# Two fused layers on one core: casts and copies of the first two units go to ScalarE, weight slabs move forward in the GpSimd queue, and the order table is replaced

## The chip, the cores and the metric

The kernel runs on one core of a Trainium2 chip. The metric is the device time of one execution in microseconds; lower is better. Besides plain timed runs there is one execution under the hardware profiler, from which all views of the trace come.

## The reference

The program computes a retention layer for 8 batches and 8 heads (576 positions, head dimension 64) and, on its output, a feed-forward layer with the gate h·cos(h).

```python
scores = scale * np.matmul(q, k.transpose(0, 1, 3, 2))
gamma = 1.0 - 2.0 ** (-5.0 - np.arange(H, dtype=np.float32))
Dmat = np.where(rel >= 0, gamma[:, None, None] ** rel[None, :, :], 0.0)
ret = scores * Dmat[None, :, :, :]
attn_out = np.matmul(ret, v)            # [8, 8, 576, 64]
x = attn_out.transpose(0, 2, 1, 3).reshape(4608, 512)
h = x @ w_in                            # [4608, 2048]
out = (h * np.cos(h)) @ w_out           # [4608, 512], float32
```

## The kernel before

**Tiles.** A unit (b, g) is batch b with positions 256·g to 256·g+255 (g = 0, 1); the last 64 positions of four batches together form a unit (x, 2). The units are worked in pairs: (0,0), (1,0), then (0,1), (1,1), then (2,0), (3,0) and so on. Each pair gives one block of 512 tokens for the feed-forward layer; there are nine blocks, j = 0 to 8.

**Attention of a unit.** SyncE loads q, k and v as float32 into `stgq`, `stgk`, `stgv` (L585, 512 KB each for the units spoken of here). Then k is cast to bf16 (`natk`, L574 on ScalarE, L575 on VectorE or GpSimd), and q and v are multiplied by decay factors while they are cast (`qnat`, `natv`, L624). Each of the three comes as two halves, y = 0 and y = 1, of 128x512 elements. For the first two pairs of units TensorE transposes `natk` and `qnat` in four-matmul groups against the identity (L648), and ScalarE or VectorE copies the result out of PSUM into `kt` and `qt`. Later units are transposed by DMA (L663). TensorE makes the scores (`bk<-qt,kt`, L694), VectorE masks them (`pt`, L743), TensorE multiplies them with `natv` (`bk<-pt,natv`), adds the product of the queries with a running 64x64 state (`bk<-qt,sba`), and updates the state (`bk<-natv,natk`). The output is copied to `xt`.

**Feed-forward.** The first product of block 0 is a sequence of four-matmul groups (L908) over the four column slabs of `w_in`, taken in the order 0, 2, 1, 3; slabs 0 and 2 are done for each half of the block apart (256 columns), slabs 1 and 3 for both halves at once (512 columns). ScalarE makes the cosine (`cb`), VectorE the product (`gt`). The second product (L1177), and the first one of blocks 3 to 8 (L1037), use a scheme with seven products of sub-blocks instead of eight.

**Weight slabs.** GpSimd requests the slabs with DMAs that convert to bf16 (`win`, L888; `wout`, L892). Each has a gate: slab 0 of `w_in` waits until q of (0,0) has landed, slab 2 until q of (1,0) has, slabs 1 and 3 until k of (1,0) has. The loads of unit (0,1) wait until slab 2 has landed. The four slabs of `w_out` wait for k of unit (1,1), and the loads of (2,0) wait for one of them.

**What sets the order.** Every step is a task on one engine. A string, `ORDER`, gives each task a rank; on each engine the tasks run in the order of rank. A planner (`Graph.run`) walks through the tasks with assumed durations. [...] `SHARES` and `FETCH` are such assumptions: shares of the DMA engines when both kinds of queue are active, and the delay with which a block of TensorE instructions becomes usable.

**The first units.** In `unit`, a unit with `fast` set, which holds for (0,0) and (1,0), casts half 0 of k on ScalarE and half 1 on GpSimd. In the loop over `tpe`, the transposed tiles of half 0 are copied by ScalarE and those of half 1 by VectorE, if the unit is fast or stands in `BOTH`; otherwise ScalarE copies all.

## Time and profile before

| | us |
|---|---|
| median of 3 runs | 283.97 |
| lowest, highest | 283.41, 285.73 |
| profiled execution | 284.13 |
| its span, first to last instruction | 282.4 |
| TensorE busy | 270.7 (96%) |
| VectorE, ScalarE, GpSimd busy | 227.3, 177.5, 161.2 |

A row of a timeline gives the start, the duration, the engine, the line, the operation with its output and inputs, the count of merged instructions, and in brackets the idle time of the engine before it with what ended that idle time. PE is TensorE's matmul, PEld its weight load, DVE is VectorE, ACT ScalarE, POOL GpSimd, SP SyncE; a q behind the name marks the engine's sequencer, which waits and issues DMAs. "issue" means that the engine waited for nothing that the profile shows. In a table of windows each row is a stretch of time with each engine's busy time and instruction count, the granted TensorE clock, the busy share of the DMA engines (it can exceed 1, since packets overlap) and what they moved in GB/s.

### The profile page before, as it was taken

What the parts mean: (1) busy time and instruction counts of PE and PEld (TensorE: products, weight loads), DVE (VectorE), ACT (ScalarE), POOL (GpSimd) and SP (SyncE); (2) the same over time, 40 slices, a digit from 0 to 9 for tenths busy, and PEclk for the clock granted to TensorE, in tenths of its full rate; (3) what the DMA queues carried; (4) which work ended last, traced back from release to release, by engine and by line L of the source; (5) the groups of instructions that cost most, each with busy time, mean ns of one, the idle gap of its engine ahead of it and who ended that gap; (6) DMA issues with size and microseconds to landing.
All of it is one profiled execution on the core that took longest, in us unless ns stands there. A gap on an engine that the chain in (4) does not pass through costs nothing.

```text
span 282.4 us, 9745 instructions
## 1 busy us (share of the span) xinstructions
PE 270.7 (96%) x4136; PEld 219.9 (78%) x4136; DVE 227.3 (80%) x394; ACT 177.5 (63%) x367; POOL 161.2 (57%) x180
## 2 busy tenths in 40 slices
PE   6779989999999999979999999999999999999995
PEld 2457568888885468868888888888888888888884
DVE  3666889988974998868997996688759899997764
ACT  4346767255247765669469875885778865778530
POOL 4640872167377683897568757981375667216330
DMA  7999999999999999999999997979816090410016
GB/s 199 249 192 262 273 171 163 300 243 263 179 187 245 204 264 206 181 221 176 251 192 208 279 238 134 168 194 175 194 32 123 6 163 2 159 69 0 2 74 224
DMA packets 122731, 49.91 MB, mean 177 GB/s; under 512 B 84800, under 2 KB 118592, under 8 KB 122688
## 3 DMA queue, kind: packets, MB, share of 16 engines
q1 hardware_dynamic: 118176, 44.84, 74.8%
q0 software_dynamic: 4224, 4.19, 9.6%
q8 instruction: 32, 0.52, 0.8%
q10 hardware_dynamic: 288, 0.26, 0.3%
q14 instruction: 11, 0.09, 0.1%
HBM read 36.70 MB, written 9.44 MB: 163 GB/s over the span
## 4 chain that ended last, share of the span: by engine, by line
PE 84%; DMA 8%; POOL 3%; issue 2%; SPq 1%; DVE 1%; ACT 1%; DVEq 0%; ACTq 0%
PE bk L1177 38%; PE bk L1037 26%; PE bk L908 11%; PE bk L694 8%; DMA stgq<-in_q_dram 3%; DMA win<-in_moe_w_in_dram 3%; DMA stgk<-in_k_dram 3%; POOL natv L624 1%; SPq L585 1%; POOL qnat L624 1%; POOL gt L1026 1%; POOL win L888 0%; ACT xt L574 0%; DVE sq L1020 0%; PE bk L648 0%
## 5 line engine op out<-in xcount | busy, mean ns | idle before, releaser
L1026 POOL TENSOR_TENSOR gt<-sq,cb 128x512 bf16<-128x512 f32 x48 | 55.8, 1172 | 49.1 <-ACT cb L1022 27.0
L908 PE MATMUL bk<-xt,win 128*128 128x256 bf16 (+1 forms) x288 | 46.3, 308 | 1.8 <-DMA win<-in_moe_w_in_dram 0.9
L624 POOL TENSOR_TENSOR natv<-stgv,wv 128x512 bf16<-128x512 f32 x36 | 37.5, 1046 | 12.5 <-DVE s L1108 4.8
L920 DVE TENSOR_TENSOR gt<-bk,cb 128x256 bf16<-128x256 f32 (+1 forms) x72 | 34.5, 507 | 12.0 <-ACT cb L917 9.3
L917 ACT ACTIVATE cb<-bk 128x256 bf16<-128x256 f32 (+1 forms) x72 | 31.2, 455 | 19.6 <-PE bk L908 16.5
L624 POOL TENSOR_TENSOR qnat<-stgq,wq 128x512 bf16<-128x512 f32 x32 | 33.5, 1052 | 16.7 <-DVE s L1114 5.6
L1037 PE MATMUL bk<-xt,win 128*128 128x256 bf16 x288 | 41.0, 273 | 0.0
L1020 DVE TENSOR_TENSOR sq<-bk,sq 128x512 f32<-128x512 f32 x48 | 32.5, 684 | 8.9 <-PE bk L1037 5.0
L908 PEld LDWEIGHTS bk<-xt,win 128*128 128x128 bf16 x288 | 26.8, 98 | 15.3 <-DVE pt L743 1.2
L743 DVE TENSOR_TENSOR pt<-bk,tr 128x512 bf16<-128x512 f32 x48 | 31.1, 682 | 8.4 <-PE bk L694 8.1
L575 POOL CAST natk<-stgk 128x512 bf16<-128x512 f32 x34 | 20.7, 614 | 28.2 <-DMA stgk<-in_k_dram 15.7
L1177 PE MATMUL bk<-wout,gt 128*128 128x256 bf16 x288 | 36.7, 273 | 0.0
L1026 DVE TENSOR_TENSOR gt<-bk,cb 128x512 bf16<-128x512 f32 x48 | 32.3, 682 | 4.0 <-ACT cb L1022 3.8
L1177 PE MATMUL bk<-wout,s 128*128 128x256 bf16 x288 | 35.6, 273 | 0.0
L1177 PE MATMUL bk<-tw,s 128*128 128x256 bf16 x288 | 35.4, 273 | 0.0
L574 ACT ACTIVATE sq<-bk 128x512 f32<-128x512 f32 x48 | 27.7, 595 | 10.0 <-PE bk L1037 8.8
L1022 ACT ACTIVATE cb<-sq 128x512 bf16<-128x512 f32 x48 | 30.0, 632 | 5.4 <-DVE sq L1020 2.9
L1022 ACT ACTIVATE cb<-bk 128x512 bf16<-128x512 f32 x48 | 28.4, 598 | 6.7 <-PE bk L1037 3.7
L1177 PEld LDWEIGHTS bk<-tw,s 128*128 128x128 bf16 x288 | 28.0, 98 | 3.6 <-DVE pt L743 0.3
L1037 PEld LDWEIGHTS bk<-xt,win 128*128 128x128 bf16 x288 | 27.9, 98 | 3.6
L1177 PEld LDWEIGHTS bk<-wout,gt 128*128 128x128 bf16 x288 | 27.6, 98 | 3.7 <-issue 0.2
L1177 PEld LDWEIGHTS bk<-wout,s 128*128 128x128 bf16 x288 | 27.7, 98 | 3.5
(80 smaller groups left out, 436.5 us busy)
## 6 DMA issues: line engine op xcount, KB each, us to landing
stgq<-in_q_dram SPq DMA_DIRECT2D x16, 512.0 KB, 6.1
out_dram<-os SPq DMA_DIRECT2D x16, 512.0 KB, 4.4
stgk<-in_k_dram SPq DMA_DIRECT2D x20, 256.0 KB, 5.6
stgv<-in_v_dram SPq DMA_DIRECT2D x20, 256.0 KB, 5.4
stgk<-in_k_dram SPq DMA_DIRECT2D x6, 512.0 KB, 6.9
stgv<-in_v_dram SPq DMA_DIRECT2D x6, 512.0 KB, 7.4
win<-in_moe_w_in_dram POOLq DMA_DIRECT2D x4, 512.0 KB, 8.0
wout<-in_moe_w_out_dram POOLq DMA_DIRECT2D x4, 512.0 KB, 7.5
```

What stands on the lines that cost most here:

```text
L574: return self.one(eng, dur, lambda e: e.activation(dst(), src(), AF.Copy), r=r, w=w, **kw)
L624: self.one(eng, 610 if eng == "dve" else 1030, lambda e, out=out, inp=inp, tab=tab, col=col, hs=hs: e.tensor_tensor(out(), inp(), ap(tab, ...
L694: return lambda e: e.matmul(out(), lhs(), rhs(), start=start, stop=True, skip_group_check=True)
L743: self.one("dve", 610, lambda e, r=r, b=b, pt=pt: e.tensor_tensor(ap(self.at(pt), 1024, 0, 128, 512 * r, [64 * ny * ny, 8 // ny // ny], [1 ...
L908: inst = e.matmul(ap(self.at(bk), 512, 0, 128, 0, [1, n]), ap(self.WIN, 4 * DFF, 0, 128, c * DFF + 128 * f, [1, 128]), ap(self.at(xt), 204 ...
L917: self.one("act", n - 15, lambda e: e.activation(ap(self.at(cb), TB, 0, 128, 0, [1, n]), ap(self.at(bk), 512, 0, 128, 0, [1, n]), AF.Sin, ...
L920: self.one("dve", 75 + n / 0.96, lambda e: e.tensor_tensor(ap(self.at(gt), NF * TB, 0, 128, f * TB + 256 * h0, [1, n]), ap(self.at(bk), 51 ...
L1020: self.one("dve", 610, lambda e: e.tensor_tensor(half(src), self.at(bank).ap(), half(src), ALU.add), r=[(bank,)], w=four(src))
L1022: self.one("act", 530 if name else 490, lambda e: e.activation(self.at(cb).ap(), ap(self.at(src), size, 0, 128, 0, [1, 512]), AF.Sin, bias ...
L1026: self.one(eng, 1120 if name else 610, lambda e: e.tensor_tensor(ap(self.at(gt), NF * TB, 0, 128, (8 * n + 2 * g) * TB + 256 * h, [TB, 2], ...
L1037: inst = e.matmul(ap(self.at(bank), 512, 0, 128, 256 * f, [1, 256]), l(c, f), rr(c), stop=True, skip_group_check=True, start=(first and f ...
L1177: inst = e.matmul(place(bank, tt), l(f, tt), rr(f), stop=True, skip_group_check=True, start=(first and f == 0 and tt < len(bank)))
```

## The change

Half 1 of k of the two fast units is cast on ScalarE instead of GpSimd. `BOTH` now lists (0,0) and (0,1), and being fast no longer counts: so the four transposed tiles of (1,0) are all copied by ScalarE, while those of (0,0) and (0,1) remain shared between ScalarE and VectorE as before. The planner's assumptions on DMA shares, slab durations and instruction fetches are changed, and the whole order table is replaced.

```diff
-    BACKLOG, FIRST = 4000, 6000
-    SHARES = (0.65, 0.30)
-    FETCH = (3200, 1500, 2550, 2000)
+    BACKLOG = 4000
+    SHARES = (0.80, 0.42)
+    FETCH = ((8000, 3200, 0, 3550), (45000, 3200, 1500, 5050), (1e9, 3200, 1500, 3250))
...
-                    usable[k] = max(a + self.FETCH[0], dma_free + self.FETCH[1]) + self.FETCH[2] + self.FETCH[3] * (a < 45000)
+                    x, y, z = next(w for end, *w in self.FETCH if a < end)
+                    usable[k] = max(a + x, dma_free + y) + z
...
     ORDER = (
-        "#####$#$#$#%#%#$#######%#&#&#%#$#&#'#)#(#'#)#,#+#'#.#7#/#*#/#'#+#*#,#(#-#.#&#&#%#*#)#(#-#(#)#*#0#2#0#1#3"
+        "#$#$###&#&#%#&#####$###%#$#%#%###$#'#(#(#)#'#*#)#*#,#@#-#.#.#'#,#+#/#-#.#,#&#'#(#*#)#+#+#(#(#)#0#1#/#0#1"
...
-    BOTH = ((0, 1),)
+    BOTH = ((0, 0), (0, 1))
...
-                    eng = ("act", "pool")[y] if fast else self.CASTS.get(u, "pp pp pp")[y]
+                    eng = "act" if fast else self.CASTS.get(u, "pp pp pp")[y]
...
-                        self.tpe(nb, 512 * y, [(y,)], t[dst], (y,), ("act", "dve")[y] if fast or u in self.BOTH else "act")
+                        self.tpe(nb, 512 * y, [(y,)], t[dst], (y,), ("act", "dve")[y] if u in self.BOTH else "act")
...
-                 sem=f"{which}{s}", dma=2750 if which == "win" else 3000, tail=900, prio=prio)
+                 sem=f"{which}{s}", dma=3350 if which == "win" else 3450, tail=500, prio=prio)
```

On GpSimd, behind the constants, these rows stand at the start before (`natk` is the cast of keys, `natv` the scaled values, `win` and `wout` the requests of weight slabs):

```order
L575 CAST natk<-stgk 128x512
L624 TENSOR_TENSOR natv<-stgv,wv 128x512
L575 CAST natk<-stgk 128x512
L624 TENSOR_TENSOR natv<-stgv,wv 128x512
L888 DMA win<-in_moe_w_in_dram 128x4x512 x2
L624 TENSOR_TENSOR natv<-stgv,wv 128x512 x2
L888 DMA win<-in_moe_w_in_dram 128x4x512 x2
```

On the same engine, at the same place, now, up to the first two requests of `w_out` slabs:

```order
L625 TENSOR_TENSOR natv<-stgv,wv 128x512 x2
L889 DMA win<-in_moe_w_in_dram 128x4x512 x3
L625 TENSOR_TENSOR natv<-stgv,wv 128x512 x2
L889 DMA win<-in_moe_w_in_dram 128x4x512
L576 CAST natk<-stgk 128x512 x2
L625 TENSOR_TENSOR qnat<-stgq,wq 128x512 x2
L625 TENSOR_TENSOR natv<-stgv,wv 128x512 x2
L893 DMA wout<-in_moe_w_out_dram 128x4x512 x2
```

The two casts are gone from the head of the queue, three slab requests stand together ahead of the values of (1,0), and the first two slabs of `w_out` are requested before any cast of unit (1,1).

On TensorE, from the second score group of (1,0) to the first product's dense stretch, before:

```order
L694 MATMUL bk<-qt,kt 64x128 x16
L908 MATMUL bk<-xt,win 128x256 x12
L517 MATMUL bk<-one 128x512 x2
L908 MATMUL bk<-xt,win 128x256 x4
L694 MATMUL bk<-pt,natv 64x128 x32
L694 MATMUL bk<-qt,sba 64x128 x4
L694 MATMUL bk<-natv,natk 64x64 x16
L694 MATMUL bk<-qt,sba 64x128 x4
L908 MATMUL bk<-xt,win 128x256 x24
```

On TensorE at the same place now:

```order
L695 MATMUL bk<-natv,natk 64x64 x16
L909 MATMUL bk<-xt,win 128x256 x12
L518 MATMUL bk<-one 128x512 x3
L695 MATMUL bk<-pt,natv 64x128 x32
L695 MATMUL bk<-qt,sba 64x128 x4
L695 MATMUL bk<-natv,natk 64x64 x16
L695 MATMUL bk<-qt,sba 64x128 x4
L909 MATMUL bk<-xt,win 128x256 x32
```

Three groups of the first product instead of four stand ahead of the output of (1,0), and 219 matmuls of the program precede its first matmul now, 224 before. The fillers are 26 in all, 24 before; all other matmuls are the same in number.

On SyncE the first two loads change places, so that k of (0,0) now comes ahead of its q, and of unit (1,1) v now comes ahead of q.

## The prediction

> **What bounds the kernel now.** I read the table of windows first, with the page's head.

> ```profile
> span 282.4 us, 9745 instructions
> ...
> 0.00:42.00 42.00, 35.12 (x515) 21.83 (x516) 28.18 (x67) 22.82 (x50) 22.74 (x42) 1.00 1.06 225
> 42.00:234.00 192.00, 190.19 (x3097) 158.09 (x3095) 161.81 (x269) 128.38 (x269) 121.11 (x124) 1.00 0.97 191
> ```

> The first number behind the stretch and its length is TensorE's busy time. From 42 to 234 us it is busy for 190.19 of 192 us: 1.81 us of idle time, 1.46 of it in a single row quoted below. In the first 42 us it is idle for 6.88 us, and part of its busy time is filler. So the time is a start plus a dense run, and a change of order pays in the start, where the DMA share is above 1. Next I read the chain of waits in the first 44 us, to see what the start waits for.

> ```profile
> 3.21 7.18 DMA stgk<-in_k_dram
> ...
> 10.45 0.61 POOL natk L575
> 11.06 1.00 POOL natv L624
> 12.06 0.89 POOL win L888
> 12.95 8.27 DMA win<-in_moe_w_in_dram
> ...
> 21.70 8.43 DMA stgq<-in_q_dram
> ...
> 30.21 1.76 POOL qnat L624 x2
> ...
> 32.23 2.05 POOL natv L624 x2
> ...
> 34.32 0.44 PE bk L694 x16
> ```

> A cast of (1,0) stands in GpSimd's queue ahead of the slab requests; the second requested slab (number 2) lands at 21.22 and releases the loads of (0,1); its queries land at 30.13; two casts follow on GpSimd. TensorE reaches the attention of (0,1) only then. Third, DMA in stretches of one microsecond:

> ```profile
> 12.00:13.00 1.00, 1.00 (x23) 0.55 (x20) 1.00 (x2) 0.38 (x1) 1.00 (x3) 1.00 1.16 282
> 13.00:14.00 1.00, 0.45 (x5) 0.15 (x4) 1.00 (x3) 0.00 (x0) 0.77 (x2) 1.00 0.77 46
> 14.00:15.00 1.00, 1.00 (x44) 0.85 (x44) 1.00 (x3) 0.71 (x2) 1.00 (x2) 1.00 0.71 91
> ...
> 24.00:25.00 1.00, 1.00 (x10) 0.75 (x8) 0.84 (x2) 0.95 (x4) 0.00 (x0) 1.00 1.21 243
> ...
> 35.00:36.00 1.00, 1.00 (x6) 0.49 (x5) 1.00 (x3) 0.31 (x2) 1.00 (x2) 1.00 0.71 208
> 36.00:37.00 1.00, 1.00 (x31) 0.47 (x32) 1.00 (x2) 0.73 (x2) 1.00 (x2) 1.00 0.77 72
> ```

> The last two numbers are DMA share and GB/s. A full microsecond shows a share of about 1.2. Two holes stand out: 13 to 15 us, between the loads of the first pair and the first slab, and 35 to 37 us, between the loads of the second pair and the first `w_out` slab.

> **The change part by part.** *GpSimd's head and the slabs.* The queue now begins with two `natv` and goes straight to three slab requests.

> ```profile
> 8.73 1.04 POOL L624 TENSOR_TENSOR natv<-stgv,wv 128x512 bf16<-128x512 f32 x1 [1.29 <-ACT qt L574]
> ...
> 12.00 1.71 POOL L888 DMA_DIRECT2D win<-in_moe_w_in_dram  x2
> 13.94 2.04 POOL L624 TENSOR_TENSOR natv<-stgv,wv 128x512 bf16<-128x512 f32 x2 [0.23 <-DMA stgv<-in_v_dram]
> 15.93 1.55 POOL L888 DMA_DIRECT2D win<-in_moe_w_in_dram  x2
> ```

> With both `natv` from 8.73, 2 x 1.04 us, the first request comes at 10.81 instead of 12.00: 1.19 us sooner. The second waits for q of (1,0): k of (1,0) lands at 3.21 + 7.18 = 10.39, and two successive loads stand 6.80 - 5.07 = 1.73 us apart at their consumers (rows below), so about 12.1, and the request goes out some 0.8 us sooner than at 12.95. Behind that wait on GpSimd are queued slab 1 (15.93 before, about 13 now) and `natv` of (1,0), which needs a landing near 13.9 anyway. That adds nothing.

> What sooner requests are worth is bounded by the holes, since the sum of bytes stays: filling 13 to 15 gives (1.2 - 0.77)/1.2 + (1.2 - 0.71)/1.2 = 0.36 + 0.41 = 0.77 us. I take **-0.8** for slab 2, and so for the loads and casts of (0,1); bounds -1.2 (the whole shift of the request) and 0 (the engines merely divide). [...]

> *The second hole.* Two `w_out` requests now stand directly behind `natv` of (0,1), which ends at 32.23 + 2.05 = 34.28, less the 0.8. The first was issued at 34.76, the second at 37.14.

> ```profile
> 34.76 0.81 POOL L892 DMA_DIRECT2D wout<-in_moe_w_out_dram  x1
> ...
> 37.14 0.80 POOL L892 DMA_DIRECT2D wout<-in_moe_w_out_dram  x1
> ...
> 43.59 0.44 PE bk L1177 x4
> ```

> The hole is worth (1.2 - 0.71)/1.2 + (1.2 - 0.77)/1.2 = 0.77 us for `w_out`. TensorE first needs it at 43.59, and the chain there comes along TensorE itself. I take half, **-0.4**; bounds -0.8 and 0. In return the casts of (1,1) wait for two requests, 0.81 + 0.80; its first transposes stand far behind, among groups of the first product of block 1.

> *Casts and copies on ScalarE.*

> ```profile
> 5.07 1.29 DVE L624 TENSOR_TENSOR qnat<-stgq,wq 128x512 bf16<-128x512 f32 x2 [1.22 <-DMA stgq<-in_q_dram]
> ...
> 6.80 0.63 ACT L574 ACTIVATE natk<-stgk 128x512 bf16<-128x512 f32 x1 [2.77 <-DMA stgk<-in_k_dram]
> ...
> 8.64 0.59 ACT L574 ACTIVATE kt<-bk 128x512 bf16<-128x512 bf16 x1
> ...
> 16.24 2.46 DVE L743 TENSOR_TENSOR pt<-bk,tr 128x512 bf16<-128x512 f32 x4
> ...
> 17.71 1.47 PE L908 MATMUL bk<-xt,win 128*128 128x256 bf16 x12 [0.88 <-DMA win<-in_moe_w_in_dram]
> ```

> For (0,0) k lands first now, so its two casts (2 x 0.63) run while q is on its way; q's two casts on VectorE (1.29) then follow a landing at 6.80 and end near 8.1, about where the transposes stood before. Cost 0. For (1,0) the second cast adds 0.63 and the second `kt` and `qt` copies 0.59 each on ScalarE: 1.8 us, of which one cast and one `qt` copy can stand ahead of its scores. Cover: the first product waits for slab 0 until 17.71 in any case. Without the cover it would cost 1.2; I take 0. (The change's name says that all copies of the first two units go to ScalarE; the diff does that for (1,0) alone.)

> *TensorE's order up to the second pair.* The output of (1,0) now stands behind 12 matmuls of the first product, not 16.

> ```profile
> 1.12 4.82 PE L517 MATMUL bk<-one 128*128 128x512 bf16 x13 [1.12 <-DVE lg L543]
> ...
> 20.40 0.50 PE L908 MATMUL bk<-xt,win 128*128 128x256 bf16 x3 [0.68 <-issue]
> 20.83 0.64 PE L694 MATMUL bk<-pt,natv 64*64 64x128 bf16 x32
> ...
> 39.57 3.22 PE L908 MATMUL bk<-xt,win 128*128 128x256 bf16 x28 [0.15 <-ACT xt L574]
> ```

> At 3.22/28, near 0.11 us each, the 4 that move behind it are 0.44 us. It started at 20.83; the earliest is when `pt` ends, 16.24 + 2.46 = 18.70. So TensorE's side of the start gains between 1.7 (2.13 - 0.44) and, if it starts at 20.40, nothing. The middle covers the 0.8 of the DMA side, so I add nothing. The opening fillers fall from 13 to 9. The 13 took 4.82 us, which is about nine at 0.43 and four at 0.22, so a burst of nine might end before the faster pace begins; 16 transposes and 32 score matmuls would then run at half pace, 0 to +0.5 us, which the wait for slab 0 covers: 0.

> *Waits without a releaser.* Besides the 0.68 at 20.40 there are two:

> ```profile
> 38.22 0.22 PE L694 MATMUL bk<-natv,natk 64*64 64x64 bf16 x3 [0.71 <-issue]
> ...
> 125.45 0.25 PE L694 MATMUL bk<-natv,natk 64*64 64x64 bf16 x7 [1.46 <-issue]
> ...
> q8 instruction: 32, 0.52, 0.8%
> ```

> The first comes behind 221 matmuls by the order's counts, the second behind 467: 246 matmuls, each with a weight load, plus some waiting instructions, so near 512 instructions. The instruction queue moved 0.52 MB in 32 packets, 16 KB each. I read these as TensorE running out of fetched instructions. [...] In the new order 219 matmuls precede the output of (1,0), so the first boundary, near the 221st, falls on its second or third matmul and not on a group of the first product; no order of 4136 matmuls avoids the others. I take **0**; bounds -2.2 (the two later gaps go) and +3.9 (below).

> *The rest of the order* is new on every engine. Idle time from 42 to 234 us is 1.81 us in all, so a gain is at most that; a loss can be of the same size: 0, bounds -0.4 (without the 1.46 counted above) and +1.8.

> Sum: -0.8 - 0.4 = -1.2 against the profiled 284.13 (span 282.4 and 1.73 around it): 282.9. The median of the runs lies 0.16 below the profiled execution: **282.8**.

> **The rivals.** *No gain: the first instruction block decides* (0.22). If it still arrives at 20.40, the output of (1,0) starts at 20.40, with 0.44 us more work behind it: the start stays, and slabs that land sooner only wait. For it: that row follows an issue gap, not a DMA. Against it: the later chain runs through slab 2 and q. Time 284.0.

> *Also the later gaps go* (0.15). -1.2 and the 0.71 and 1.46: 284.13 - 3.37 - 0.16 = 280.6. For it: both fell into bursts of small matmuls, which an order can spread. Against it: the new order still has such bursts for every pair.

> *Slower: the first block comes after the slabs* (0.07). Three slab requests in a row keep the DMA engines full (1.2) from 12.5 us on, without the hole at 13 to 15 in which a fetch finds room. The slabs leave the queue near 25, as the row 24:25 (still 1.21) shows. If the block arrived only then, the output of (1,0) would start near 24.7 instead of 20.83: +3.9, and all attention behind it is late: 284.13 + 3.9 - 0.16, near 287.9. It decides as soon as the block arrives after about 21.6 (20.83 and the 0.8 won). Against it: before, a block arrived in the middle of the slabs, by 20.40.

> *A little slower: the new dense run is worse* (0.11). Two more gaps like the 1.46, or late casts, +1.5 to +2.9 against -1.2: 284.3 to 285.7.

> **How the numbers follow.** The forecast, 282 to 283.7, has 0.45; the rivals have 0.55 as given. The range 280.7 to 285.6 leaves out half of the second rival, all of the third and a little of the fourth. I call 1% what a measurement of this kernel can tell from no change, as its three runs span 0.8%: 281.1 and 286.8. Faster than that: most of the second rival and a trace of the forecast, 0.13. Slower: the third and a trace of the fourth, 0.09. Within: 0.78.

> **What the changed profile would show.** The first slab request near 10.8; no hole of DMA share at 13 to 15; slab 2 landing near 20.4 and q of (0,1) near 29.3; the first `w_out` request near 33.5; the output of (1,0) between 18.7 and 20.4; issue gaps behind about 221 and 467 matmuls; TensorE busy for some 190 of 192 us from 42 on. The prediction is wrong if the loads of (0,1) come sooner and its scores do not (first rival), if the first issue gap ends after 21.6 (third), or if the time differs beyond 42 us.

## The result and the profile after

| | us |
|---|---|
| changed kernel, median of 17 runs | 286.19 (284.23 to 288.48) |
| kernel before, median of 17 runs beside it | 283.60 (282.32 to 285.73) |
| ratio, 95% interval | 1.0098 (1.0075 to 1.0121) |
| profiled execution, and its span | 288.41, 286.5 |

The change makes the kernel 2.6 us slower. That is above the predicted range, and the profile shows where. The windows of the changed kernel, in the columns of the prediction's table:

```profile
0.00:42.00 42.00, 35.95 (x519) 21.79 (x520) 27.13 (x66) 25.13 (x55) 23.43 (x42) 1.00 1.09 228
42.00:234.00 192.00, 188.08 (x3002) 155.23 (x3000) 159.96 (x266) 126.44 (x264) 117.92 (x119) 0.99 0.92 191
```

From 42 to 234 us TensorE is idle for 3.92 us where it was 1.81, and the granted clock, 1.00 before, is 0.99. The start does not explain the loss, as far as this trace goes. The timeline of the start of the changed kernel, GpSimd and then TensorE:

```profile
10.84 0.96 POOL L889 DMA_DIRECT2D win<-in_moe_w_in_dram  x1
12.62 1.49 POOL L889 DMA_DIRECT2D win<-in_moe_w_in_dram  x2 [0.83 <-DMA stgq<-in_q_dram]
...
17.46 1.48 PE L909 MATMUL bk<-xt,win 128*128 128x256 bf16 x12 [0.53 <-DVE xt L576]
...
19.52 0.74 PE L695 MATMUL bk<-pt,natv 64*64 64x128 bf16 x32
...
28.57 0.38 PE L649 MATMUL bk<-idn,natk 128*128 128x128 bf16 x4 [0.72 <-POOL natk L576]
```

The first slab is requested at 10.84 (12.00 before), the output of (1,0) starts at 19.52 (20.83), and the gaps without a releaser at 20.40 and 38.22 are gone. But the first product starts only 0.25 us sooner (17.46 after 17.71), and TensorE now waits 0.72 us at 28.57 for the key cast of (0,1). What TensorE waits for at 17.46 is no longer the slab, which landed at 17.18 (17.57 before), but the copy of attention output to `xt` on VectorE, which ended at 17.40. Compare the two traces at equal work of TensorE's matmuls (columns times the share of the array that a matmul uses; fillers, the matmuls on a tile of ones, `bk<-one`, left out): the new kernel is some 0.6 us ahead at 5 us of work, 0.2 ahead at 35, within 0.2 of level at 125 and 3.5 behind at 135. That last step is one place, near 168 us of the trace (the profiled execution, 288.41, is the second slowest of the 17, so it shows more of the loss than the median does). TensorE around it, and below it three windows, in whose rows the granted clock is the third number from the right:

```profile
165.94 0.30 PE L695 MATMUL bk<-natv,natk 64*64 64x64 bf16 x13
168.37 0.19 PE L695 MATMUL bk<-natv,natk 64*64 64x64 bf16 x1 [2.12 <-issue]
...
169.68 3.40 PE L1178 MATMUL bk<-tw,s 128*128 128x256 bf16 x16
...
168.00:170.00 2.00, 1.63 (x23) 1.29 (x23) 0.80 (x2) 1.21 (x2) 0.83 (x2) 0.83 1.38 122
170.00:172.00 2.00, 2.00 (x11) 1.40 (x10) 1.81 (x3) 0.00 (x0) 1.99 (x3) 0.50 1.28 115
172.00:175.00 3.00, 3.00 (x27) 2.55 (x25) 0.75 (x2) 1.45 (x3) 0.72 (x1) 0.88 1.12 275
```

TensorE stops for 2.12 us in the middle of a group, waiting for nothing that the profile shows, and then runs at half clock: 16 matmuls take 3.40 us. Counting matmuls, weight loads and waits in the trace, the stopped matmul is TensorE's instruction 5313, one short of 450 + 19 x 256 = 5314. The gaps of the kernel before stand at 450, 961 and 3778, that is at k = 0, 2 and 13 of the series 450 + 256k (450, 962, 3778; to one). The trace also holds the fetch itself. The instruction queue moved 32 packets of 16 KB, one for about every 256 of TensorE's instructions (8276 matmuls and weight loads, and some hundred waits); the one that belongs to this place (the 20th) ran from 165.76 to 167.07, and TensorE went on 1.30 us after its end. For the gap of 0.62 us at 125.56 it is the 14th packet, to 124.02: 1.54 us.

A smaller loss lies near 107 us. VectorE, GpSimd and TensorE there:

```profile
104.65 2.35 DVE L962 TENSOR_TENSOR xs<-xt 128x512 bf16<-128x512 bf16 x1
...
104.60 2.13 POOL L945 TENSOR_TENSOR tx<-win 128x1024 bf16<-128x1024 bf16 x1
...
107.06 0.61 PE L1038 MATMUL bk<-xs,tx 128*128 128x256 bf16 x4 [0.51 <-DVE xs L962]
...
109.67 2.79 PE L1178 MATMUL bk<-tw,s 128*128 128x256 bf16 x24 [0.49 <-DVE s L1109]
```

The next `xs` of VectorE, of the same size, takes 0.42 us. This one took 2.35, and ended 0.27 us after GpSimd's operation of 2.13, which started 0.05 us ahead of it. In the kernel before that operation of GpSimd ended at 104.00, ahead of VectorE's sums.

### The profile page after: what moved, and what is told of

Read it like the earlier page. It is cut to its first block, busy times and chain, and to the rows that moved or that the text cites. A ratio compares the mean times of both kernels' runs of the same rounds, so it can differ in the third digit from the quotient of the medians.

```text
span 286.5 us, 9742 instructions
## 1 busy us (share of the span) xinstructions
PE 273.3 (95%) x4138; PEld 220.6 (77%) x4138; DVE 225.8 (79%) x392; ACT 179.6 (63%) x371; POOL 161.0 (56%) x178
## 4 chain that ended last, share of the span: by engine, by line
PE 84%; issue 5%; DVE 4%; DMA 3%; POOL 2%; SPq 1%; DVEq 0%; POOLq 0%
PE bk L1178 38%; PE bk L1038 26%; PE bk L909 11%; PE bk L695 8%; DMA stgq<-in_q_dram 3%; SPq L586 1%; DVE xs L962 1%; DVE pt L744 1%; POOL win L889 1%; POOL natv L625 1%; PE bk L649 1%; DVE s L1109 1%; DVE gt L921 1%; DVE xt L576 0%; POOL natk L576 0%
## 5 line engine op out<-in xcount | busy, mean ns | idle before, releaser
L921 DVE TENSOR_TENSOR gt<-bk,cb 128x256 bf16<-128x256 f32 (+1 forms) x72 | 33.8, 507 | 12.8 <-ACT cb L918 10.8
L1027 DVE TENSOR_TENSOR gt<-bk,cb 128x512 bf16<-128x512 f32 x48 | 32.5, 684 | 12.1 <-ACT cb L1023 11.3
L576 POOL CAST natk<-stgk 128x512 bf16<-128x512 f32 x32 | 19.7, 626 | 37.1 <-DVE s L1115 14.2
L1178 PE MATMUL bk<-tw,s 128*128 128x256 bf16 x288 | 36.6, 280 | 0.5 <-DVE s L1109 0.5
L1178 PE MATMUL bk<-wout,s 128*128 128x256 bf16 x288 | 36.2, 273 | 0.0
L575 ACT ACTIVATE sq<-bk 128x512 f32<-128x512 f32 x48 | 28.1, 598 | 7.7 <-PE bk L1038 6.9
L1178 PEld LDWEIGHTS bk<-tw,s 128*128 128x128 bf16 x288 | 28.6, 101 | 5.3 <-DVE s L1109 1.1
```

What stands on the lines that cost most here:

```text
L575: return self.one(eng, dur, lambda e: e.activation(dst(), src(), AF.Copy), r=r, w=w, **kw)
L921: self.one("dve", 75 + n / 0.96, lambda e: e.tensor_tensor(ap(self.at(gt), NF * TB, 0, 128, f * TB + 256 * h0, [1, n]), ap(self.at(bk), 51 ...
L1027: self.one(eng, 1120 if name else 610, lambda e: e.tensor_tensor(ap(self.at(gt), NF * TB, 0, 128, (8 * n + 2 * g) * TB + 256 * h, [TB, 2], ...
L1178: inst = e.matmul(place(bank, tt), l(f, tt), rr(f), stop=True, skip_group_check=True, start=(first and f == 0 and tt < len(bank)))
```

## The experiments

Three theories. **F** (fetch): TensorE's instructions come in blocks of 256, and it runs out of them at 450 + 256k, the boundaries between blocks; the new order lets such a boundary fall where the next block comes late. **D** (late operands): the new order lets VectorE and GpSimd collide, and TensorE waits. **S** (start): the new start costs something. Every kernel was timed beside the kernel before on the same chip, and ratios are against that.

| run | median us | before us | ratio (95%) |
|---|---|---|---|
| e1 changed kernel again | 287.45 | 283.71 | 1.0120 (1.0080 to 1.0159) |
| e2 new start, old rest | 283.38 | 283.71 | 0.9984 (0.9960 to 1.0008) |
| e3 old start, new rest | 286.74 | 283.71 | 1.0104 (1.0075 to 1.0133) |
| e4 changed, boundaries moved by 24 | 284.68 | 283.71 | 1.0035 (1.0007 to 1.0063) |
| e5 changed, one difference on VectorE | 284.97 | 283.01 | 1.0078 (1.0050 to 1.0106) |
| e6 before, boundaries moved by 24 | 288.30 | 283.01 | 1.0183 (1.0163 to 1.0203) |
| e7 e4 and e5 together | 283.25 | 283.01 | 1.0003 (0.9987 to 1.0020) |
| e8 e2, boundaries moved by 24 | 283.40 | 283.01 | 1.0006 (0.9990 to 1.0023) |
| e9 changed, five loads cut | 286.16 | 283.13 | 1.0117 (1.0092 to 1.0141) |
| e10 as e7, moved by 18 | 284.62 | 283.13 | 1.0028 (0.9994 to 1.0063) |
| e11 as e8, casts back on GpSimd | 285.79 | 283.13 | 1.0100 (1.0073 to 1.0127) |
| e12 changed, all DMA of 157 to 170 us cut | 284.70 | 283.20 | 1.0043 (1.0019 to 1.0067) |

**Which part loses (e1, e2, e3).** The changed kernel ran again. Then the order table was spliced: the first 273 or 274 of the 1477 steps (to about 55 us) from one kernel, the rest from the other; e2 has the changed kernel's casts and copies, e3 those of before.

> The changed kernel unaltered, beside the others on the same chip, with a second profile. Theory F (TensorE runs out of fetched instructions at certain places of the new dense order, and its clock falls afterwards): about 286, and the profile again shows issue gaps behind matmuls 1850 and 2613 of 4138, perhaps shorter, since the gap depends on when the block comes. Theory S (the start): about 286, with the start late. Theory D (operands that come late in the new dense order, from VectorE or ScalarE): about 286, with the lost time spread over many short gaps whatever the issue gaps do.

> The changed kernel with the new order for the first 274 of 1477 tasks (to about 55 us) and the order of before for the rest. Theory F: 283.3, since the start is 0.2 to 0.3 us ahead in the trace and the dense run is that of before again. Theory S: about 286. Theory D: 283.3, as theory F.

> The kernel before, with its engines and planner's numbers, its order for the first 273 tasks and the new order for the rest. Theory F: about 286, with an issue gap near the same matmuls as in the changed kernel. Theory S: 283.6. Theory D: about 286.

The new rest with the old start loses 1.04%, the new start with the old rest loses nothing. S falls: the loss lies in the new dense order. In the profile of e3 the long gap is there again, 1.36 us at 167.94, while `xs` takes 0.43 us, since GpSimd's operation had ended by then: so the collision comes and goes with the timing.

**Boundaries moved, the order unchanged (e4).** 12 small matmuls stand behind the opening fillers, in time that was idle. They add 24 instructions to TensorE's stream and change nothing else.

```diff
             for _ in range(n):
                 inst = e.matmul(self.at(self.wb).ap(), self.ONE.ap(), ...)
+            for _ in range(tiny):
+                inst = e.matmul(ap(self.at(self.wb), 512, 0, 32, 0, [1, 32]), ap(self.ONE, 128, 0, 128, 0, [1, 32]),
+                                ap(self.ONE, 128, 0, 128, 0, [1, 32]), start=True, stop=True, skip_group_check=True)
+        tiny, self.TINY = self.TINY, 0
...
+    TINY = 12
```

> The changed kernel with 12 small filler matmuls (32 columns, 32 weights) behind the opening fillers, where TensorE waits anyway; each is a weight load and a matmul, so every later instruction stands 24 places further on, and the boundaries between blocks of 256 instructions fall 12 matmuls earlier in the work. Nothing else changes. Theory F: the gaps of 0.80 and 2.31 us behind matmuls 1850 and 2613 go or shrink, the granted clock stays at 1.000, and the time falls to 283.3 to 284.5, if the new places are no worse. Theory S and theory D: within 0.3 us of the changed kernel, about 286.

The ratio falls from 1.0120 to 1.0035, some 2.4 us (0.0085 x 283). The matmul that had waited 2.12 us follows its neighbours at once. The packet of the block began at 159.99 instead of 165.76: it came 5.8 us sooner, while TensorE passed the instruction 322 ahead of the boundary 1.3 us sooner (157.80 after 159.11). (From that instruction the kernel's planner counts a fetch, in `Graph.run`; that the chip does so is not shown.) TensorE in e4, at the same matmuls as above:

```profile
165.59 0.31 PE L699 MATMUL bk<-natv,natk 64*64 64x64 bf16 x14
165.84 0.31 PE L699 MATMUL bk<-qt,sba 64*64 64x64 bf16 x12
```

**The collision alone, and both (e5, e7).** One of GpSimd's differences, the one at 104.60, goes to VectorE and stands just ahead of `xs` in its order. TensorE's instructions stay as they are.

```diff
+                eng = "dve" if (i, c) == (1, 1) else eng
                 self.one(eng, 2150 if eng == "pool" else 660, lambda e, i=i, c=c, x=x, y=y: e.tensor_tensor(...),
```

> The changed kernel with one of GpSimd's 128x1024 differences (tx, the one that ran 104.60 to 106.73 beside VectorE's xs of 2.35 us) done by VectorE just ahead of that xs; TensorE's instructions and their order are the same. Theory D (late operands: VectorE slowed by GpSimd): xs takes 0.42 us again, both waits of TensorE, 0.51 near 107 and 0.49 near 110 us, go or nearly so, and the time falls by 0.8 to 1.3 us, to about 286.2 (against 287.45 of the changed kernel in its last five rounds). Theory F (fetch gaps): nothing of the loss behind 160 us changes: the gap of about 2 us at TensorE instruction 5313 stays; if F is all, the time stays at 287.4.

> The changed kernel with both edits: the 12 small matmuls that moved the boundaries (284.68 alone), and the difference on VectorE. If F and D are separate losses they add: no gaps at 450 + 256k beyond 1 us, xs at 0.42 us, and 284.68 less 0.8 to 1.3, so 283.4 to 283.9, no different from the kernel before. If the moved boundaries had already taken what D costs: 284.7.

VectorE and TensorE in e5:

```profile
104.93 0.41 DVE L963 TENSOR_TENSOR xs<-xt 128x512 bf16<-128x512 bf16 x1
...
106.29 0.60 PE L1039 MATMUL bk<-xs,tx 128*128 128x256 bf16 x4
...
107.16 3.66 PE L1179 MATMUL bk<-tw,s 128*128 128x256 bf16 x32
...
165.29 0.31 PE L695 MATMUL bk<-qt,sba 64*64 64x64 bf16 x12 [1.04 <-PE bk L695]
```

`xs` takes 0.41 us, both waits are gone, and a gap stays at the boundary (instruction 5314; the row names PE as releaser, but the block's packet ended 1.27 us ahead of this matmul, as with the other gaps). D is worth 0.9 us (e4 to e7, 0.0032 x 283) to 1.2 us (e1 to e5, 0.0042 x 283), F 2.1 us (e5 to e7) to 2.4 us. F is clear of the noise; for D alone the intervals of e1 and e5 overlap, and those of e4 and e7, so its size rests also on the two waits, 0.51 + 0.49 = 1.00 us. Against the first measurement of the changed kernel (1.0098 in place of 1.0120) e4 and e5 would give 1.8 and 0.6 us. With both edits the new order is level with the old one, and its dense run has 0.49 us of idle time (the profiled execution is the fastest of the twelve, 282.05):

```profile
42.00:234.00 192.00, 191.51 (x3111) 159.32 (x3109) 164.75 (x274) 130.27 (x271) 119.75 (x123) 1.00 0.90 190
```

**The same edit on the kernel before (e6).**

> The kernel before with 12 small matmuls (24 TensorE instructions, 0.5 us) behind the opening fillers, inside an idle time of 1.54 us; nothing else. Theory F: the gaps stand at instructions 450 + 256k, so the gap of 1.46 us no longer stands at the same matmul of 125 us, where the block boundary now falls into a slower stretch; the time falls by 1.0 to 1.6 us, to about 282.4, unless the boundary near 152 us, which now falls into a faster stretch, opens a gap of its own (then about 283.7). The rival (the gap belongs to the operations there, a late operand that the trace does not show): the gap stays at the same matmul, 283.7.

It costs 5.2 us (0.0183 x 283), although every engine's order is that of the kernel before. Neither a gain nor 283.7 came true. The gap at 125 us did leave its matmul, as F says, but for one that stands twelve matmuls earlier in the order, and the early boundaries became worse (0.68 to 1.83 and 0.71 to 1.21 us). TensorE in e6, and two windows:

```profile
18.03 0.49 PE L912 MATMUL bk<-xt,win 128*128 128x256 bf16 x3 [1.16 <-DMA win<-in_moe_w_in_dram]
20.34 1.47 PE L912 MATMUL bk<-xt,win 128*128 128x256 bf16 x9 [1.83 <-issue]
...
41.55 0.21 PE L698 MATMUL bk<-qt,sba 64*64 64x128 bf16 x1 [1.21 <-issue]
...
128.23 0.22 PE L698 MATMUL bk<-qt,kt 64*64 64x64 bf16 x3 [1.25 <-issue]
...
20.00:22.00 2.00, 1.66 (x10) 1.15 (x11) 0.00 (x0) 0.15 (x1) 0.00 (x0) 0.76 1.20 192
22.00:24.00 2.00, 2.00 (x30) 1.14 (x32) 0.85 (x2) 1.17 (x4) 0.00 (x0) 0.50 1.23 202
```

The three gaps stand at instructions 450, 961 and 3778, the same numbers as before, on other matmuls. The boundary is tied to the count, not to an operation. After the first of them, half clock again.

In this profile the loss arises at the first boundary: compared at equal work, e6 is 3.1 us behind at 10 us of work (26 us of the trace before), and 2.7 at the end. The block does not come later than before, TensorE goes on at 20.34 (20.40 before); but the boundary stands twelve matmuls earlier, so that less work is done when it is reached, and the gap and the half clock follow. The profiled execution, 286.86, is the fastest of the six. The mean granted clock of the others goes down to 0.982.

**The new start with moved boundaries (e8), and another distance (e10).**

> The new first 274 steps with the old rest (283.38, with a gap of 1.79 us at instruction 3777) and the 12 small matmuls. Theory F: the gap at 3777 goes, 283.38 - 1.8 = 281.6, faster than the kernel before. The rival: the gap stays with its matmul, 283.4.

> The changed kernel with the difference on VectorE and 9 instead of 12 small matmuls (18 instructions instead of 24). Theory F: the shortest stretches between the request of a block and its first use get a little longer than with 12 (6.7 instead of 6.4 us for the third and fourth shortest), so the time is equal to that of the run with 12 (283.25, ratio 1.0003) or up to 0.5 us shorter, 282.8 to 283.3. If a place and not the boundary decided, the gap near 165 us would be back: 285.

Neither forecast of F came true; the times are near those of the rivals (283.4 and 285), but the gaps did not stay with their matmuls, they stand at boundaries. In the profiles of e2 and e8 the gap at instruction 3777 shrank; TensorE in e2, then in e8:

```profile
126.20 0.28 PE L695 MATMUL bk<-natv,natk 64*64 64x64 bf16 x10 [1.60 <-issue]
```

```profile
124.79 0.25 PE L699 MATMUL bk<-qt,kt 64*64 64x64 bf16 x6 [0.45 <-issue]
```

But the ratios 0.9984 and 1.0006 overlap. The profiled execution of e2, at 284.85 us, was the slowest of its twelve (from 282.90), so its gap need not be that of most of them. e10 shows the same more plainly: of its twelve executions five took 282.1 to 283.5 us and seven 284.6 to 286.2. The profiled one is of the second kind (285.1) and has the gap, on instruction 5314:

```profile
166.53 0.28 PE L699 MATMUL bk<-natv,natk 64*64 64x64 bf16 x9 [2.21 <-issue]
```

That the other five had no gap is likely, but they have no trace. Two traces of one program do show it: the changed kernel has the gap of 0.62 us at 125.56, and e1, the same program, has none there (its packet ended at 123.80, and the matmul came at 125.96). So whether a block comes in time differs between executions of one program.

**What makes the block late (e9, e12).**

> The changed kernel, with five loads of 256 KB (keys and values, issued between 159.74 and 162.80 us in the profile of the changed kernel) cut to 16 of their 128 partitions: the last units are computed from old data. No instruction of TensorE and no order changes. Theory F in its sharper form (the instruction block that TensorE needs at 168 us is fetched through the same DMA engines and waits there behind those loads): the gap of about 2 us at instruction 5313 shrinks to 0.5 us or less, no half clock follows there, and the time falls by about 2 us, to some 285.0 on a day on which the changed kernel has 287. If the fetch has a fixed latency that no traffic lengthens, the gap stays at 1.2 to 2.3 us and the time with it.

> The changed kernel with all DMA between about 157 and 170 us cut to an eighth: the five loads of the run before, the two stores of the output (512 KB each) and the two transposes; one block of the output is mostly not written, the last units are computed from old data. TensorE's instructions are the same. With the five loads alone cut, the gap at instruction 5313 was 1.66 us, and the block came right behind the second store. If the fetch waits for DMA traffic, whatever its kind, the gap goes (0.3 us or less) and the time falls by 2 us or more, to a ratio near 1.004 with the kernel before. If the fetch is late by itself (requested late, or slow without traffic), the gap stays at 1.2 to 2.3 us and the ratio near 1.010.

In both, the edit cuts single DMAs to an eighth, by a partition count or, for the transposes, a count of blocks:

```diff
+            n0, n = n, n // 8 if len(self.G.tasks) in self.LIGHT else n
...
+                p, rows = 16, [[DM, 16]] + rows[1:]
...
+            m = 1 if len(self.G.tasks) in self.LIGHT else 8
```

The sharper form of F fails in e9: with the five loads cut to an eighth the gap stays. TensorE in e9, and at the same matmuls in e12:

```profile
167.79 0.19 PE L696 MATMUL bk<-natv,natk 64*64 64x64 bf16 x1 [1.48 <-issue]
```

```profile
166.60 0.44 PE L697 MATMUL bk<-natv,natk 64*64 64x64 bf16 x14
166.86 0.31 PE L697 MATMUL bk<-qt,sba 64*64 64x64 bf16 x12
```

With the stores and transposes cut as well it goes, and the ratio falls from 1.0120 (e1) to 1.0043. So DMA traffic has a part in the delay, though that of the loads has little. Which of the two kinds does it, store or transpose, was not tried. Nor is it the whole: counted from TensorE's instruction 4992, 322 ahead of the boundary, the packet began after 6.6 us in the changed kernel, 6.5 in e9 and still 4.5 in e12 (2.2 in e4), and in e12 TensorE passed the boundary without a gap 1.20 us after its packet's end. Why the packet comes so late while the DMA engines are nearly free (a share of 0.49 or less from 160 us on in e12) stays open. These are one profile each. One window each, e9 and e12, between 165 and 166 us:

```profile
165.00:166.00 1.00, 1.00 (x52) 0.76 (x53) 1.00 (x3) 1.00 (x3) 0.14 (x1) 1.00 2.93 135
```

```profile
165.00:166.00 1.00, 1.00 (x11) 0.90 (x10) 1.00 (x3) 0.88 (x4) 0.90 (x1) 1.00 0.04 2
```

The DMA engines are claimed nearly threefold in e9 at only 135 GB/s, while a transpose stands in the queue; in e12 they are free. The packet ran from 165.51 to 166.44 in e9 and from 164.37 to 165.49 in e12.

**The casts alone (e11).** Against e8, the two casts go back to the head of GpSimd's queue.

```diff
-                    eng = "act" if fast else self.CASTS.get(u, "pp pp pp")[y]
+                    eng = ("act", "pool")[y] if fast else self.CASTS.get(u, "pp pp pp")[y]
```

> The new first steps with the old rest and moved boundaries (283.40, ratio 1.0006), with the two key casts put back on GpSimd at the head of its queue, as before; three more fillers and three fewer small matmuls, so that the boundaries stay where they are. The first slab request goes out near 11.9 instead of 10.85. By the prediction's largest term (the requests fill the hole of DMA share, 0.8 us) slab 2 lands 0.8 us later and the time rises by 0.8, to about 284.2. By what the start showed in the runs (all of the new start is worth 0.2 to 0.45 us) the time rises by 0.4 at most, 283.4 to 283.8.

It costs 2.7 us (0.0094 x 283), more than either side expected. GpSimd and TensorE, in e11 and then in e8:

```profile
12.14 2.46 POOL L893 DMA_DIRECT2D win<-in_moe_w_in_dram  x3
...
19.41 1.47 PE L913 MATMUL bk<-xt,win 128*128 128x256 bf16 x12 [0.89 <-DMA win<-in_moe_w_in_dram]
```

```profile
10.78 0.96 POOL L893 DMA_DIRECT2D win<-in_moe_w_in_dram  x1
...
17.51 1.47 PE L913 MATMUL bk<-xt,win 128*128 128x256 bf16 x12 [0.63 <-DMA win<-in_moe_w_in_dram]
```

Requested at 12.14 with two more slabs directly behind it, the first slab lets TensorE start at 19.41. In the kernel before it was requested at 12.00, with one slab behind it and the third only after two `natv`, and TensorE started at 17.71. So with three requests in a row the first slab takes 1.6 us longer ((19.41 - 12.14) - (17.71 - 12.00)), and the sooner request just pays for that. This is read from the three traces and was not tried by itself. The first product starts 1.9 us later than in e8 (19.41 - 17.51), and at equal work 1.75 us of that stays behind the start. The rest of the lag in its profile, 3.7 us in all (an execution of 287.66 us, above the median of 285.79), comes from gaps of 0.87 us at 82.83 and 1.55 at 128.45 (0.45 in e8), both at boundaries. So the 2.7 us are in part this chance of the boundaries, and what the casts alone cost was not separated from it.

## Why the prediction was wrong

*The time.* 282.8 was predicted, with a range to 285.6; the median is 286.19.

*The step that failed: the waits without a releaser.* Their cause was read rightly, as instruction blocks that come late, and their distance too: "near 512 instructions". The step "no order of 4136 matmuls avoids the others", from which the term was taken at 0, is where it went wrong; no run shows that 0. In the changed kernel's trace most boundaries cost nothing, one 0.62 us and one 2.12. The last went when the boundaries were moved by 24 instructions (e4), and when the DMAs of 157 to 170 us were cut (e12); a new order deals these places anew. In all fourteen profiles every gap of 0.25 us or more at a boundary that no late operand explains ends 1.2 to 1.6 us after the packet of its block. Instead of the 1.46 us at 125 the new order has 0.62 there and 2.12 at 168, followed by half clock, a cost that the term had not. Measured by moving the boundaries alone, and clear of the noise: 2.1 to 2.4 us. The term's upper bound, +3.9, held; it was used for the first block only.

*The rest of the order*, taken at 0 with a bound of +1.8, costs 0.9 to 1.2 us through one collision of GpSimd with VectorE.

*The start*, -1.2, was too large: e2 shows -0.45 us (0.0016 x 283; by its interval -1.1 to +0.2). The steps themselves are in the trace. The first request went out at 10.84 (10.8 predicted), the output of (1,0) started at 19.52 (between 18.7 and 20.4), and the hole at 13 to 15 us is filled, as two windows of the changed kernel show:

```profile
13.00:14.00 1.00, 1.00 (x59) 0.91 (x48) 0.82 (x2) 0.12 (x1) 1.00 (x2) 1.00 1.32 216
14.00:15.00 1.00, 0.86 (x10) 0.37 (x7) 0.00 (x0) 0.76 (x2) 0.99 (x2) 1.00 1.16 170
```

What lacks is the step from landings to TensorE. The keys of (0,1) are cast at 27.82 and TensorE stands before them at 27.85, with matmuls of the first product behind it that it could have run. That the order was drawn up for still sooner loads is likely, but not shown. The landings came as forecast: slab 2 at 20.43 (near 20.4 predicted, 21.22 before), q of (0,1) at 29.57 (29.3; 30.13). The second hole's -0.4 found no place either: the first request of `w_out` went out at 33.65 (33.5 predicted), but the DMA share from 35 to 36 us is 0.53 (0.71 before), and the lead, 0.2 us at 35 us of work, is 0.2 at 60 too.

*Casts and copies on ScalarE*, 0: nearly right, since the output of (1,0) came sooner and not later. But its cover, the wait for slab 0, was gone: ScalarE's `qt` copies hold the scores of (1,0) until 15.38, VectorE stands 2.26 us before their mask with the `xt` copy behind it, and the first product starts 0.28 us after slab 0 has landed (17.46, 17.18). The casts that left GpSimd are worth 1.36 us of the first request (12.14 in e11, 10.78 in e8), in place of the 1.19 predicted.

*The rivals.* The nearest was the last, "a little slower: the new dense run is worse", with a chance of 0.11 and "two more gaps like the 1.46, or late casts". It names the mechanism, but as either, and without the half clock; both together lie above its 285.7. "Also the later gaps go" came true for 0.71 and in part for 1.46, now 0.62; but a new gap stands at 168.37. The first-block rivals did not happen here. The third has the fetch find room in the hole at 13 to 15 us; in the kernel before, the first packet ran from 18.04 to 18.98, at a DMA share of 1.23. e6 comes near the third of them by another road: its output of (1,0) starts at 23.45 with a block that is no later than before.

*The boundaries.* Every gap of 0.25 us or more here that no late operand explains stands at 450 + 256k, to one instruction. Of some thirty boundaries (8276 matmuls and weight loads by 256) two have such a gap in the profile of the changed kernel, of 0.62 and 2.12 us.

## What to carry to other kernels

An order is part of the program's timing beyond what precedes what: in a stream of thousands of small matmuls, count instructions, mark every 256th (the gaps here stood at 450 + 256k), and look at what stands ahead of the mark, which DMAs run there, and when the instruction queue's packet for it lands. A change of order, or of a few fillers, should be judged against a copy of itself with the boundaries shifted, since the shift alone moved the time of these kernels by -0.85 to +1.8%. And a sooner landing is worth only what the consumer's order can use (slab 2 landed 0.79 us sooner, 20.43 after 21.22, and e2 gained 0.45); look at what the engine reaches first.

## What the hardware showed

```profile
165.89:169.30 3.41, 1.28 (x63) 1.07 (x48) 1.84 (x4) 1.04 (x2) 1.60 (x2) 1.00 1.42 244
169.30:172.72 3.42, 3.42 (x19) 2.38 (x17) 2.04 (x4) 0.64 (x2) 2.71 (x3) 0.50 1.04 127
```

```profile
162.62:166.04 3.42, 1.70 (x62) 1.30 (x59) 2.68 (x6) 1.84 (x4) 1.51 (x2) 1.00 1.24 276
166.04:169.45 3.41, 2.92 (x45) 2.49 (x46) 2.25 (x4) 1.21 (x2) 2.12 (x4) 1.00 1.36 128
```

In the changed kernel the whole gap lies in one stretch; in e10 the grid cuts it into 1.71 and 0.50, in e1 into 0.43 and 1.43. In the thirteen traces that have such moments (the kernel before has none), from the first of them to the trace's end, a stretch with 2.09 us or more of idle TensorE was followed by half clock each time, and none with 1.91 us or less was (in the changed kernel those with 2.12 and 2.09 were, and none of those with 1.27 or less); most of the former lie at the kernel's end, and in mid-run there are two, 2.12 here and 2.23 in e6. Of the changed kernel's 17 executions, six have a mean granted clock of 0.994 or less and average 287.4 us, the other eleven 285.8. The difference, 1.6 us, is about what one stretch at half clock costs by the windows (1.7), so the clock explains part of the loss and of the spread, not the whole. TensorE was busy throughout from 150 to 165 us, ahead of the gap, at full clock (15.00 of 15.00 us, 1.00).

**A short VectorE operation that takes as long as GpSimd's.** `xs` took 2.35 us beside GpSimd's operation of 2.13, which had started 0.05 us sooner; the next `xs` took 0.42, and in e5, without GpSimd's operation beside it, this one took 0.41. In the changed kernel, e1 and e9 `xs` starts 0.05, 0.13 and 0.43 us behind GpSimd's operation, and ends 0.27 to 0.28 us after it each time. What makes VectorE wait is not shown.
